# Half-array down products among the first queries and scores of a fused attention and GeGLU kernel

## The chip, the cores and the metric

The kernel runs on one core of a Trainium2 chip. The metric is the time of one execution on the device in microseconds (us). Engines are named TensorE (PE in the profile, its weight loads PEld), VectorE (DVE), ScalarE (ACT), GpSimd (POOL) and SyncE (SP); SyncE here only starts DMA transfers.

## The reference

For 2048 tokens of width 448: a layer norm, then two branches from the same normed rows, and a gated sum.

```python
xn = _layernorm(x, axis=-1)
# A: 16 query heads, 8 key/value heads, Dh = 256, the last W = 512 keys
q = (x @ wq).reshape(B, Sq, Hq, Dh).transpose(0, 2, 1, 3)
scores = jnp.einsum("bhqd,bhkd->bhqk", q, k) * (Dh ** -0.5)
o = jnp.einsum("bhqk,bhkd->bhqd", _softmax(scores, axis=-1), v)
s = o.transpose(0, 2, 1, 3).reshape(B, Sq, Hq * Dh) @ wo
# B: 448 -> 1792 -> 448
g = _silu((_gelu(xn @ w_gate) * (xn @ w_up)) @ w_down)
return x + s * g
```

## The kernel before, in words

**FFN.** The 2048 tokens are 16 tiles of 128, four tiles to a chunk of 512 columns. `gu_group` (L543) makes gate and up of 128 hidden features for one chunk, as pairs of 64-row products in the two row halves of TensorE; `gu_evac` (L558) takes them out of PSUM (gelu on ScalarE into `gl`, the product with up on VectorE into `actT[c % 2][:, f, :]`, f = 0 to 13). A down tile is 14 full 128-row products of `actT` and `wd`, 448 columns wide, into one PSUM bank (`down_mm`, L572), then the gate: tanh on ScalarE, `(tanh + 1) * sum` on VectorE (`down_gate`, L577), which `store_g` (L567) sends to DRAM by SyncE's queue. `down_tile` (L588) does a whole tile; `down` (L592) does tiles 0 to 3 and 4 to 7 among the gate and up groups. Tiles 8 to 15 are cut into pieces of 4 to 7 products by `down_piece` (L997) and set between the products of value and output weights of each head (`vw_head`, L732). Tile 14 sums in bank 0, tile 15 in bank 3.

**Attention.** The value cache times the output weights of each head is made beforehand (`vw`), so that a step only has to make queries, scores, softmax and `p @ vw`. There are 128 steps n: 8 blocks c of 256 queries, 16 heads h = n % 16 each. In step n TensorE makes the scores of step n (`s_jobs`, two tiles t, banks 4 to 6 in turn), the queries of step n + 2 (`q_jobs`; bank 7, and for steps 2 to 5 the second half of the head in bank 1) and the products with `vw` of step m = n - 4 (`pv_jobs`, `pv_plan`), as soon as n is 4. All of these are products of 64 rows; each list has a lower and an upper half (u = 0, 1), and `halves` (L799) merges the two lists by their columns so that both row halves of TensorE are fed in turn. TensorE takes its queue in order. Where one half writes a bank that the other half wrote before, `halves` makes it wait for the other's last product there.

The product with `vw` uses seven products in place of eight (a Strassen form). Its inputs are the transposed probabilities `pT` and four sums of them, `sS[0]` to `sS[3]`, that VectorE makes in the order 0, 2, 1, 3 (`sums`, L882). `AT` and `B0` to `B3` say which product goes to which of banks 0 to 3: product 7 reads `sS[2]`, product 6 reads `sS[1]`, both go to bank 1 (`B1`); product 3 reads `sS[3]` and goes to bank 3 (`B3`). The upper half of an ordinary step is queries, scores, then B1, B3, B2, B0; the lower half is the first scores, B0 and B2, queries, the second scores, B1, B3. `FIRST`, `LAST` and `TLAST` name the products that start and end a bank's sum.

The other engines run through the rest of a step in the order of the program (L1052 to L1117): VectorE's reciprocal of step n - 1 and GpSimd's two norms `pn`, a transposing DMA into `pT` by SyncE's queue, VectorE's row minimum of each tile (`row_min`), ScalarE's copy of the new queries (`q_evac`; in steps 0 to 3 VectorE copies the second half of the head from bank 1), ScalarE's exponential of each tile (`expo`), VectorE's sums of step n - 3. In the step where a block ends (h = 3, m % 16 == 15) the four banks are copied out (`evac`) and 13 end pieces (`finish`, L957: adds on GpSimd, multiplies with the gate on VectorE) are put on a list, from which each step takes one at its end (L1111).

**Around the change.** After the heads' `vw`: the queries of steps 0 and 1 in two calls of `halves` (L1026, L1027), a piece of four down products (L1051), and in each of steps 0 to 3 a piece of five at the step's end (L1098). Tile 14 ends in step 1, tile 15 in step 3; `store_g` comes at the start of steps 2 and 4 (L1057).

Of the kernel before, what the change touches and what calls it, by code (L numbers as in the profile page):

```python
# [13 lines left out]
P = 128  # L14
# [152 lines left out]
def bass_recurrent_scan__sliding_block_cached__geglu_ffn__prompt_kernel(  # L167
# [12 lines left out]
    _, S, D = A_x.shape  # L180
    Hkv, Sk, Dh = A_k_cache.shape[1], A_k_cache.shape[2], A_k_cache.shape[3]
    HD = A_wq.shape[1]
    Hq = HD // Dh
    W = min(4096, max(256, Sk // 4))
    F = B_w_gate.shape[1]
    NT = S // P
    QC = 512
    NQC = S // QC
    NF = F // P
    NJ = W // P  # L190
    NCO = HD // P
    R = 64
# [11 lines left out]
    with es:  # L204
# [367 lines left out]
        def down_mm(t, o, wr, f0, f1):  # L572
            c, t4 = divmod(t, 4)
            mms([(o, actT[c % 2][:, f, t4 * P:(t4 + 1) * P], wd[:, f, :], f == 0, f == NF - 1)
                 for f in range(f0, f1)], [b_wd] + b_actT[c % 2], wr)

        def down_gate(t, o, wr):  # L577
            s, y = t % 2, t % NG2
# [7 lines left out]
            keep_g.append((t, g, bg))  # L586

        def down_tile(t, o, wr):  # L588
            down_mm(t, o, wr, 0, NF)
            down_gate(t, o, wr)  # L590

        def down(c, pairs):  # L592
# [139 lines left out]
        def vw_head(h, banks, last=True):  # L732
            K.reuse(flat(b_vw[h]))
            for j, i in zip((0, 2, 1, 3), banks):
                vw_mm(h, j, i)
            if last:
                vw_sums(h)
# [61 lines left out]
        def halves(lo, up):  # L799


            t, todo = [0, 0], (list(lo), list(up))
            while todo[0] or todo[1]:
                u = 0 if todo[0] and (not todo[1] or t[0] <= t[1]) else 1
                i, c0, c1, l, r, st, sp, reads = todo[u].pop(0)
                t[u] += c1 - c0 + 6
                other = half_of[i][1 - u]
                half_of[i][u] = mms([(bank[i][:, c0:c1], l, r, st, sp)], reads, [b_ps[i]],
                                    [] if other is None else [other])
# [3 lines left out]
        def q_jobs(n, e):  # L813

            c, h = divmod(n, Hq)
            y, i = c % 2, bq(n)
            if e == 1 and 2 <= n < 2 + LAG:
                i = 1
            out = ([], [])
            for u in range(2):  # L820
                rows = slice(R * u, R * u + R)
                for k in [2, 1, 0] + ([NK] if u == e else []):
                    l = wqr[rows, h, :] if k == NK else wq[rows, k, h * Dh + e * P:h * Dh + (e + 1) * P]
                    out[u].append([i, e * CW, (e + 1) * CW, l, xq[rows, y, k, :], False, False,
                                   b_wql[h // HG] + [b_xq[y][k]]])
            return out
# [14 lines left out]
        def s_jobs(n, t, low_first):  # L841
            h, i = n % Hq, bs(n, t)
            s, g = n % NQT, h // 2
            out = ([], [])
            for u in range(2):
                rows = slice(R * u, R * u + R)
                for e in range(2):
                    out[u].append([i, 0, W, qT[rows, s, e, t * P:(t + 1) * P], kT[rows, g, e, :], False, False,
                                   [b_kT[g], b_qT[s][e]]])
            flag(*((out[0], out[1]) if low_first else (out[1], out[0])))  # L850
            return out

        def row_min(n, t):
            i = bs(n, t)
            m = (2 * n + t) % 8
            K.op("dve", lambda e: e.tensor_reduce(mn[:, m:m + 1], bank[i], AX.X, ALU.min), (b_ps[i],), (b_mn[m],))  # L856
# [25 lines left out]
        def sums(n, parts):  # L882
# [7 lines left out]
            for p in parts:  # L890
# [2 lines left out]
            return o  # L893

        AT = {1: (0, 0), 2: (0, 1), 6: (1, 0), 7: (1, 1), 4: (2, 0), 5: (2, 1), 3: (3, 0)}
        B0, B1, B2, B3 = (((1, 0), (1, 1), (2, 0), (2, 1)), ((6, 0), (6, 1), (7, 0), (7, 1)),
                          ((4, 0), (4, 1), (5, 0), (5, 1)), ((3, 0), (3, 1)))
        FIRST = {(0, (1, 0)), (0, (4, 0)), (0, (3, 0)), (1, (7, 0))}
        LAST = {(1, (2, 1)), (0, (7, 1)), (1, (5, 1)), (1, (3, 1))}
        TLAST = {(0, (2, 1)), (1, (7, 1)), (0, (5, 1)), (1, (3, 1))}  # L900

        def pv_src(n):
            x, y = n % NPT, n % NSS
# [15 lines left out]
        def pv_plan(n):  # L919
            if n % Hq == Hq - 1:  # L920
                one, mid, two, all_ = B0 + B2 + B1[:1], B3, B1[1:], B0 + B1 + B2 + B3
            elif n % Hq == 0:
                one, mid, two, all_ = B0 + B2, (), B3 + B1, B0[:2] + B1[2:] + B1[:2] + B0[2:] + B2 + B3
            else:
                one, mid, two, all_ = B0 + B2, (), B1 + B3, B1 + B3 + B2 + B0
            last = LAST if n % Hq == Hq - 1 else TLAST if n == NST - LAG - 1 else ()
            u = 0 if n + LAG + 2 < NST else 1
            return [pv_jobs(n, u, x, last) for x in (one, mid, two)] + [pv_jobs(n, 1 - u, all_, last)]
# [68 lines left out]
        def down_piece(n):  # L997
            while n:
                t, f = divmod(down_at[0], NF)
                k = min(n, NF - f)  # L1000
                i = 4 + t % 2 if t < NT - 2 else (0, 3)[t - NT + 2]
                down_mm(t, bank[i][:, 0:D], [b_ps[i]], f, f + k)
                down_at[0] += k
                n -= k
                if f + k == NF:
                    down_gate(t, bank[i][:, 0:D], [b_ps[i]])
                    if t < NT - 2:
                        store_g()
# [11 lines left out]
        vw_head(14, (1, 2, 3, 6))  # L1020
        down_piece(4)
        vw_head(15, (7, 1, 2, 3))
        js = [[q_jobs(n, e) for e in range(2)] for n in range(2)]
        js[0][0][1][0][5] = js[1][1][0][0][5] = True
        js[0][0][0][-1][6] = js[1][1][1][-1][6] = True
        halves(js[1][1][0] + js[1][0][0], js[0][0][1] + js[0][1][1])  # L1026
        halves(js[0][1][0] + js[0][0][0], js[1][0][1] + js[1][1][1])  # L1027
        K.reuse(flat(b_qT))
        for n in range(2):
            q_evac(n)  # L1030
# [17 lines left out]
            act(gsl[:, t, :], gr[:, y, :], ACT.Copy, (b_gr[y], b_sc), (b_gsl[t],), scale=sc[:, 1:2])  # L1048

        todo, stores, ready = [], [], []  # L1050
        down_piece(4)  # L1051
        for n in range(NST):  # L1052
            h, m = n % Hq, n - LAG
            c = n // Hq
            more = n + 2 < NST
            ends = m >= 0 and m % Hq == Hq - 1
            if n in (2, LAG):  # L1057
                store_g()
            if n == LAG:
                K.reuse(b_pT[3:] + b_sS[2])  # L1060
            s0, s1 = s_jobs(n, 0, True), s_jobs(n, 1, not more or m < 0)
            for t in ready:
                store_out(t)
            ready, stores = stores, []
            if moves and n < NST - 2:
                moves.pop(0)()
            if more:
                q0, q1 = q_jobs(n + 2, 0), q_jobs(n + 2, 1)
                q0[1][0][5] = q1[0][-1][6] = True
                if m < 0:  # L1070
                    q1[1][0][5] = q0[0][-1][6] = True
            if m < 0:
                halves(s0[0] + s1[0] + q0[0] + q1[0], q0[1] + q1[1] + s0[1] + s1[1])
            else:
                one, mid, two, all_ = pv_plan(m)
                if more:
                    halves(s0[0] + one + q0[0] + q1[0] + mid + s1[0] + two, q0[1] + q1[1] + s0[1] + s1[1] + all_)
                else:
                    halves(s0[0] + s1[0] + all_, one + s0[1] + s1[1] + two)
            if n >= 1:  # L1080
                recip(n - 1)
                norm(n - 1)
            row_min(n, 0)
            if more:
                q_evac(n + 2)
            if ends:
                evac(0, "dve")
                evac(2, "act")
            row_min(n, 1)
            expo(n, 0)  # L1090
            expo(n, 1)
            if 3 <= n < NST - 1:
                sums(n - 3, (0, 1))
                if ends:
                    evac(1, "dve")
                sums(n - 3, (2, 3))
            if n < LAG:
                down_piece(5)  # L1098
            if n in VW12:
                vw_plain(VW12[n])  # L1100
            if n == NST - 2:
                gates_scaled(0)
                gates_scaled(1)
            if n == LAG:
                K.reuse(b_aS + flat(b_tmp) + flat(b_ofin) + b_xr + b_gr)
                for t in range(NXR):
                    load_fin(t)
            if ends:
                evac(3, "act")
                todo.extend(finish(m // Hq, "pool"))  # L1110
            for _ in range(2 if n - NST + Hq in (8, 12) else 1):  # L1111
                if todo:
                    todo.pop(0)()
            if h == LAG and c >= 1 and c + 1 < NC:
                for k in range(NK + 1):
                    moves.append(lambda k=k, y=(c + 1) % 2, d=xnd[c + 1, :, k, :], r=b_xnd[2 * c + 2:2 * c + 4]: dma(
                        "sp", xq[:, y, k, :], d, r, (b_xq[y][k],)))  # L1117
# [120 lines left out]
```

## Time and profile before

| what | value |
|---|---|
| median of 3 runs | 555.11 us (554.72 to 555.96) |
| profiled execution, its own time | 554.54 us |
| its span, first to last instruction | 552.7 us |
| mean granted TensorE clock | 0.999 |
| TensorE busy | 545.0 us (99% of the span) |
| VectorE, ScalarE, GpSimd busy | 84%, 61%, 45% |
| full 128-row down products (`bank<-wd,actT`) | 224, 353 ns mean in the record |
| attention steps, first score to first score | 2.97 us in most |

A record of a product lasts longer than its share of TensorE, since products overlap in the pipe; the pace is read from start to start. In the timelines the columns are the start, the time taken, the engine, the line, the operation, output and input by the program's names, shapes, the number of instructions merged into the row (x), and in brackets the idle time before and what ended it. In the list of waits each row says who waited for whom, how long in all, how often, and the longest.

### The profile page before, as it was taken

What the parts mean: (1) busy time and instruction counts of PE and PEld (TensorE: products, weight loads), DVE (VectorE), ACT (ScalarE), POOL (GpSimd) and SP (SyncE); (2) the same over time, 40 slices, a digit from 0 to 9 for tenths busy, and PEclk for the clock granted to TensorE, in tenths of its full rate; (3) what the DMA queues carried; (4) which work ended last, traced back from release to release, by engine and by line L of the source; (5) the groups of instructions that cost most, each with busy time, mean ns of one, the idle gap of its engine ahead of it and who ended that gap; (6) DMA issues with size and microseconds to landing.
All of it is one profiled execution on the core that took longest, in us unless ns stands there. A gap on an engine that the chain in (4) does not pass through costs nothing.

```text
span 552.7 us, 18715 instructions
## 1 busy us (share of the span) xinstructions
PE 545.0 (99%) x7612; PEld 437.2 (79%) x7612; DVE 464.7 (84%) x1202; ACT 339.8 (61%) x809; POOL 249.8 (45%) x388
## 2 busy tenths in 40 slices
PE   8999999999999999999999999999999999999996
PEld 5544444445557999999999999999999999999983
DVE  6674979858867778988988898898989989889996
ACT  5432323467766666766767666676676666666753
POOL 1121590100004444655656456555555555564665
PEclk9999999999999999999999999999999999999999
DMA  9997999501106865556656875755677476576665
GB/s 270 184 239 147 210 317 179 115 1 36 46 8 102 140 114 88 103 96 116 116 105 104 132 101 95 121 114 107 107 118 107 93 135 108 94 114 115 94 103 86
DMA packets 190246, 66.07 MB, mean 120 GB/s; under 512 B 169408, under 2 KB 187984, under 8 KB 190160
## 3 DMA queue, kind: packets, MB, share of 16 engines
q1 hardware_dynamic: 186928, 56.96, 59.6%
q0 software_dynamic: 2464, 7.34, 4.5%
q8 instruction: 60, 0.98, 0.8%
q10 hardware_dynamic: 768, 0.57, 0.3%
q14 instruction: 26, 0.21, 0.1%
HBM read 19.76 MB, written 5.77 MB: 46 GB/s over the span
## 4 chain that ended last, share of the span: by engine, by line
PE 91%; DVE 5%; DMA 2%; issue 1%; ACT 1%; POOL 0%; SPq 0%; DVEq 0%; ACTq 0%
PE bank L387 91%; DVE mn L856 1%; DVE actT L562 1%; DMA x<-in_A_x_dram 1%; DMA pT<-pn 1%; DVE mx L679 1%; DVE sS L892 1%; DVE xn L460 0%; DVE stats L434 0%; ACT gl L381 0%; POOL rstd L446 0%; SPq L375 0%; ACT p L861 0%; DVE qT L832 0%; DVE p L1121 0%
## 5 line engine op out<-in xcount | busy, mean ns | idle before, releaser
L387 PE MATMUL bank<-kT,qT 64*128 64x512 bf16 x1024 | 281.4, 376 | 0.2
L877 POOL TENSOR_SCALAR pn<-p,rd 128x512 f16<-128x512 f32 x254 | 172.5, 691 | 225.6 <-DVE rd L867 225.6
L387 PE MATMUL bank<-vw,sS 64*128 64x224 f16 x1984 | 223.3, 256 | 0.2 <-DVE sS L892 0.2
L387 PE MATMUL bank<-xq,wq 64*128 64x256 bf16 x1536 | 221.9, 269 | 0.1
L387 PE MATMUL bank<-vw,pT 64*128 64x224 f16 (+1 forms) x1520 | 208.7, 258 | 0.7 <-DMA pT<-pn 0.7
L856 DVE TENSOR_REDUCE mn<-bank 128x1 f32<-128x512 f32 x256 | 173.7, 682 | 36.8 <-PE bank L387 34.6
L861 ACT ACTIVATE p<-bank,mn 128x512 f32<-128x512 f32 x256 | 174.9, 684 | 5.3 <-DVE mn L856 2.5
L387 PEld LDWEIGHTS bank<-vw,sS 64*128 64x128 f16 x1984 | 164.1, 94 | 7.9 <-DVE sS L892 2.5
L387 PEld LDWEIGHTS bank<-xq,wq 64*128 64x128 bf16 x1536 | 141.7, 94 | 10.0 <-PE bank L387 0.7
L381 ACT ACTIVATE qT<-bank 128x512 bf16<-128x512 f32 (+1 forms) x128 | 75.5, 590 | 117.1 <-PE bank L387 116.3
L387 PEld LDWEIGHTS bank<-vw,pT 64*128 64x128 f16 (+1 forms) x1520 | 142.5, 94 | 5.8 <-DMA pT<-pn 1.4
L387 PEld LDWEIGHTS bank<-kT,qT 64*128 64x128 bf16 x1024 | 95.1, 94 | 4.1 <-ACT p L861 1.5
L892 DVE TENSOR_TENSOR sS<-pT 128x256 f16<-128x256 f16 x248 | 86.3, 388 | 0.0
L387 PE MATMUL bank<-xnT,wgu 64*128 64x512 bf16 (+2 forms) x768 | 84.5, 350 | 0.8 <-DVE actT L562 0.3
L387 PE MATMUL bank<-xq,wqr 64*128 64x256 bf16 x256 | 68.4, 269 | 0.0
L387 PEld LDWEIGHTS bank<-xnT,wgu 64*128 64x128 bf16 x768 | 36.5, 94 | 38.5 <-issue 1.1
L381 ACT ACTIVATE gl<-bank 128x512 bf16<-128x512 f32 x56 | 33.1, 597 | 49.7 <-PE bank L387 41.2
L562 DVE TENSOR_TENSOR actT<-bank,gl 128x512 bf16<-128x512 f32 x56 | 37.4, 685 | 16.7 <-PE bank L387 16.0
L861 ACT ACTIVATION_READ_ACCUMULATOR p<-bank,mn 128x1 f32 x256 | 50.7, 198 | 0.0
L387 PE MATMUL bank<-wd,actT 128*128 128x448 bf16 x224 | 45.9, 353 | 0.6 <-DVE actT L562 0.5
L892 DVE TENSOR_TENSOR sS<-pT,sS 128x256 f16<-128x256 f16 x124 | 36.2, 292 | 4.3
L387 PEld LDWEIGHTS bank<-wd,actT 128*128 128x128 bf16 x224 | 21.3, 98 | 22.1 <-issue 1.5
(84 smaller groups left out, 421.6 us busy)
## 6 DMA issues: line engine op xcount, KB each, us to landing
wq<-in_A_wq_dram POOLq DMA_DIRECT2D x8, 384.0 KB, 7.7
woa<-in_A_wo_dram POOLq DMA_DIRECT2D x6, 448.0 KB, 5.7
pT<-pn SPq DMA_TRANSPOSE x129, 3.1
xn_t<-xnT SPq DMA_DIRECT2D x16, 128.0 KB, 3.7
xr<-in_A_x_dram SPq DMA_DIRECT2D x16, 112.0 KB, 2.6
gr<-gate_t SPq DMA_DIRECT2D x16, 112.0 KB, 2.7
out_dram<-ofin SPq DMA_DIRECT2D x16, 112.0 KB, 2.0
wd<-in_B_w_down_dram SPq DMA_DIRECT2D x1, 1568.0 KB, 7.9
```

The source lines that it names most:

```text
L381: K.op("act", lambda e, o=o, i=i: e.activation(o, i, func, scale=scale), reads, writes)
L387: ins = e.matmul(o, lhsT=l, rhs=r, start=st, stop=sp)
L562: K.op("dve", lambda e: e.tensor_tensor(actT[c % 2][:, f, :], bank[b + 1], gl[:, s, :], ALU.mult), (b_ps[b + 1], b_gl[s]), (b_actT[c % 2][ ...
L679: K.op("dve", lambda e: e.tensor_reduce(mx[:, i:i + 1], o, AX.XY, ALU.max, apply_absolute_value=True), (b,), (b_mx,))
L856: K.op("dve", lambda e: e.tensor_reduce(mn[:, m:m + 1], bank[i], AX.X, ALU.min), (b_ps[i],), (b_mn[m],))
L861: K.op("act", lambda e: e.activation(p32[:, z, :], bank[i], ACT.Exp, bias=mn[:, m:m + 1], scale=-1.0, accum_out=rsum[:, 2 * r + t:2 * r + ...
L877: K.op(engs[t], lambda e, o=o, i=i, s=s: e.tensor_scalar(o, i, s, 1.0, op0=ALU.mult, op1=ALU.mult), (b_p32[z], b_rd[r]), (b_pn[y][t],))
L892: o = K.op("dve", lambda e, i=i, a=a, b=b, f=f: e.tensor_tensor(s[i], a, b, f), r, (b_sS[y][i],))
```

## The change

Five things, with their lines in the kernel before.

1. `down_mm` waits only for the `actT` buffers of its own f, and `down_tile` calls it in two groups (12 and 2 products).
2. The products of f = 4 to 13 of tile 14 and all of tile 15 become 64-row products (`d_jobs`) in the lists of `halves`: one share with the first queries, one in each of steps 0 to 3. The two calls of `halves` for the first queries become one. The pieces at L1051 and L1098 go.
3. In steps 0 to 3 the lower half makes its second scores at its end, after the queries. The gates of tiles 14 and 15 stand between the two exponentials of steps 2 and 3, `store_g` moves to steps 3 and 4, and in step 3 the four sums of step 0 are spread between the row minima, the query copy and the exponentials.
4. `B1` begins with product 7 (`sS[2]`) in place of product 6 (`sS[1]`).
5. No end piece is taken in steps with h = 4; in the last block two are taken at h = 8, 10 and 12 (before: 8 and 12).

```diff
@@ down_mm, down_tile
-                 for f in range(f0, f1)], [b_wd] + b_actT[c % 2], wr)
+                 for f in range(f0, f1)], [b_wd] + b_actT[c % 2][f0:f1], wr)
...
-            down_mm(t, o, wr, 0, NF)
+            down_mm(t, o, wr, 0, NF - 2)
+            down_mm(t, o, wr, NF - 2, NF)
@@ banks
-        B0, B1, B2, B3 = (((1, 0), (1, 1), (2, 0), (2, 1)), ((6, 0), (6, 1), (7, 0), (7, 1)),
+        B0, B1, B2, B3 = (((1, 0), (1, 1), (2, 0), (2, 1)), ((7, 0), (7, 1), (6, 0), (6, 1)),
...
-        LAST = {(1, (2, 1)), (0, (7, 1)), (1, (5, 1)), (1, (3, 1))}
-        TLAST = {(0, (2, 1)), (1, (7, 1)), (0, (5, 1)), (1, (3, 1))}
+        LAST = {(1, (2, 1)), (0, (6, 1)), (1, (5, 1)), (1, (3, 1))}
+        TLAST = {(0, (2, 1)), (1, (6, 1)), (0, (5, 1)), (1, (3, 1))}
@@ pv_plan, h = 0
-                one, mid, two, all_ = B0 + B2, (), B3 + B1, B0[:2] + B1[2:] + B1[:2] + B0[2:] + B2 + B3
+                one, mid, two, all_ = B0 + B2, (), B3 + B1, B0[:2] + B1 + B0[2:] + B2 + B3
@@ before the steps
+        def d_jobs(u, t, f0, f1):
+            rows, (c, t4) = slice(R * u, R * u + R), divmod(t, 4)
+            return [[(0, 3)[t - NT + 2], 0, D, actT[c % 2][rows, f, t4 * P:(t4 + 1) * P], wd[rows, f, :],
+                     u == 1 and t == NT - 1 and f == 0, u == 1 and f == NF - 1, [b_wd, b_actT[c % 2][f]]]
+                    for f in range(f0, f1)]
+
+        DL = ((NT - 2, 4, 10), (NT - 2, 10, NF), (NT - 1, 0, 5), (NT - 1, 5, 10), (NT - 1, 10, NF))
+        DU = ((NT - 1, 0, 6), (NT - 1, 6, 10), (NT - 2, 4, 9), (NT - 2, 9, NF), (NT - 1, 10, NF))
         js = [[q_jobs(n, e) for e in range(2)] for n in range(2)]
-        js[0][0][1][0][5] = js[1][1][0][0][5] = True
-        js[0][0][0][-1][6] = js[1][1][1][-1][6] = True
-        halves(js[1][1][0] + js[1][0][0], js[0][0][1] + js[0][1][1])
-        halves(js[0][1][0] + js[0][0][0], js[1][0][1] + js[1][1][1])
+        for q0, q1 in js:
+            q0[1][0][5] = q1[0][-1][6] = True
+        low, up = [sum([q[u] for x in js for q in x], []) for u in range(2)]
+        halves(d_jobs(0, *DL[0]) + low, up + d_jobs(1, *DU[0]))
...
-        down_piece(4)
@@ the steps
-            if n in (2, LAG):
+            if n in (3, LAG):
                 store_g()
-            s0, s1 = s_jobs(n, 0, True), s_jobs(n, 1, not more or m < 0)
+            s0, s1 = s_jobs(n, 0, True), s_jobs(n, 1, not more)
...
-                halves(s0[0] + s1[0] + q0[0] + q1[0], q0[1] + q1[1] + s0[1] + s1[1])
+                halves(s0[0] + d_jobs(0, *DL[n + 1]) + q0[0] + q1[0] + s1[0], q0[1] + q1[1] + s0[1] + s1[1] + d_jobs(1, *DU[n + 1]))
...
             row_min(n, 0)
+            if n == 3:
+                sums(0, (0,))
             if more:
                 q_evac(n + 2)
...
             row_min(n, 1)
+            if n == 3:
+                sums(0, (1, 2))
             expo(n, 0)
+            if n in (2, 3):
+                i = (0, 3)[n - 2]
+                down_gate(NT - 4 + n, bank[i][:, 0:D], [b_ps[i]])
             expo(n, 1)
-            if 3 <= n < NST - 1:
+            if n == 3:
+                sums(0, (3,))
+            elif 3 < n < NST - 1:
                 sums(n - 3, (0, 1))
...
-            if n < LAG:
-                down_piece(5)
...
-            for _ in range(2 if n - NST + Hq in (8, 12) else 1):
+            for _ in range(0 if h == LAG else 2 if n - NST + Hq in (8, 10, 12) else 1):
```

## The prediction

> **What bounds the kernel now.** I read the page's busy shares first, then the chain of waits, then the timelines around the three places that the change touches. TensorE is busy 99% of the span, and the chain lies on it:
>
> ```profile
> PE 545.0 (99%) x7612; PEld 437.2 (79%) x7612; DVE 464.7 (84%) x1202; ACT 339.8 (61%) x809; POOL 249.8 (45%) x388
> PE 91%; DVE 5%; DMA 2%; issue 1%; ACT 1%; POOL 0%; SPq 0%; DVEq 0%; ACTq 0%
> ```
>
> So the question is where TensorE is not at its pace. Starts of successive products give the pace: 64-row products of 512 columns start every 0.216 us in each row half, those of 256 columns every 0.109, those of 224 every 0.096; full 128-row products of 448 columns every 0.189 (56 of them from 38.57 to 48.98). An ordinary attention step has in each half 4, 7 and 14 of the narrow ones: 0.86 + 0.77 + 1.34 = 2.97 us, and steps 6 to 18 take just that. There is nothing to win there. Off the pace are these.
>
> *FFN.* The second row of down tiles starts late; the waits put it down to VectorE:
>
> ```profile
> 64.36 0.68 DVE L562 TENSOR_TENSOR actT<-bank,gl 128x512 bf16<-128x512 f32 x1
> ...
> 65.09 0.49 PEld L387 LDWEIGHTS bank<-wd,actT 128*128 128x128 bf16 x4 [1.04 <-DVE actT L562]
> ```
>
> The last 512-column product before it starts at 64.18; the first down product at 65.10, 0.92 later. At the first row of tiles, which waits for nothing, that distance is 0.31 (38.26 to 38.57): 0.216 for the product, 0.093 to go from half-array to full-array products. The stall is 0.61 us.
>
> *Head of attention (157 to 178).* Full down products stand between half products, and each change of form costs:
>
> ```profile
> 161.73 1.12 PE L387 MATMUL bank<-wd,actT 128*128 128x448 bf16 x5
> 162.78 0.39 PE L387 MATMUL bank<-kT,qT 64*128 64x512 bf16 x1
> ```
>
> Five products at 0.189 are 0.95, the piece takes 1.05; about 0.1 goes at either end. Steps 0, 1 and 2 take 2.79 each, step 3 takes 3.37, because VectorE and ScalarE stand behind the gate of tile 14 (step 1).
>
> *Every 16 steps.* Starts of the steps around a block's end: 219.32, 222.39, 225.49, so step 20 takes 3.07, step 21 takes 3.10. The second excess is a wait for VectorE's sums:
>
> ```profile
> 222.73 1.16 DVE L892 TENSOR_TENSOR sS<-pT 128x256 f16<-128x256 f16 x2
> ...
> 223.04 0.69 POOL L963 TENSOR_TENSOR aS<-aS 128x224 f32<-128x224 f32 x1
> ...
> 223.81 0.28 DVE L892 TENSOR_TENSOR sS<-sS,pT 128x256 f16<-128x256 f16 x1
> ```
>
> Two sums took 1.08 us start to next start (0.40 in a quiet step, 216.56 to 216.96) while GpSimd ran an end piece. The third, done at 224.09, releases TensorE at 224.14, which could have started at 224.05 in the upper half and 224.02 in the lower.
>
> **A. Down in two groups (L588, L575).** The first 12 products now wait only for their own `actT` buffers (f up to 11, done at 61.5), the last 2 for f = 12 and 13, done at 65.04; they come 12 x 0.189 = 2.27 after 64.48. Banks: the first tile's was freed by the gelu of 61.31, the second's by VectorE at 63.93. Cover is ample: **-0.61**. What is late next? From 65 to 75 VectorE has 9.5 us of work in 11, but TensorE needs none of it until the next pair of banks. VectorE is late again at 105.05, at the end of a run of work fed by TensorE after 79.08; that run starts earlier by the same 0.61. Were it held by loads instead, up to 0.36 would come back at 105.
>
> A rule speaks on the down products. In rows, LDWEIGHTS of 98 ns stands inside the 0.189 pace of full products: nothing of it shows. The Trainium skill, "TensorE: Matmul & The Clock Gate", Part 3 (The mechanism), says that a weight load overlaps a running product only where the row group differs. By that an estimate would add 24 x 0.098 = 2.4 us of gain for the half products; the row denies it, and the sum takes none.
>
> **B. Half products (L1023 to L1098).** Removed: 24 full products (4 before step 0, 5 in each of steps 0 to 3), five changes of form each way, and the drain between the two groups of first queries (157.93 to 158.26, of which 0.22 is idle). Added: 24 products in each half, at 0.189 (no 64-row product of 448 columns is in the trace; bounds 0.096 of 224 and 0.216 of 512 columns; the full one has as many columns, so its pace). If the two halves did not run side by side it would be 24 x 0.189 = 4.5 us more; the 512-column products do.
> The first stage has per half 14 x 0.109 + 6 x 0.189 = 2.66, from 157.05, less what the upper half loses waiting for bank 7 (read by VectorE until 157.21, next product at 157.26): end 159.93. The first score waits for ScalarE's queries: last lower query about 159.04, ScalarE 0.30 after it (158.93 to 159.23 before), 0.60 long: step 0 at 160.00, as before, with two pairs more done.
> Steps 0 and 3: 4 x 0.216 + 7 x 0.109 + 4 x 0.189 = 2.39; steps 1 and 2, with five: 2.575. If nothing waits, step 4 starts at 160.00 + 9.92 = 169.92 instead of 171.73.
> What is late next, with these rows: row minimum 0.69 (0.60 to the next in a busy queue), expo 0.69 with 0.81 to VectorE's reciprocal, qT on VectorE 0.41, sum 0.20 to 0.31, tanh 0.53, gate 0.62. Reciprocals fall at 164.13, 166.71 and, since tanh of tile 14 (ends 168.84) stands ahead of the last expo of step 2, 169.62. Queries of the upper half in steps 2 and 3 find bank 1 read with hardly 0.01 to spare. Then on VectorE: minimum 169.70, first sum 170.30, qT, second minimum, two sums, gate of tile 15, last sum.
> The first sum now meets GpSimd's norms (169.9 to 171.26). The nearest row is the pair above, slowed by 0.68; nothing at best, 0.96 if both norms go first; I take 0.3, the rest of one norm. The Trainium skill, "SBUF — State Buffer", section "SBUF: two separate sides", has it that VectorE and GpSimd share a port pair as an exclusive lock and that the loser waits for the whole instruction. That is a rule against this place; by it the wait would be 0.28 or 0.96, and the head's gain 1.1 or about 0.5.
> Step 4 then waits thrice: 0.1 for bank 7 (ScalarE's qT ends 169.96), 0.2 for the second sum (172.0) at the upper half's first product in bank 1, 0.5 for the last sum (173.07) and the gate of tile 15 (172.86) at the lower half's first in bank 3, due at 172.62. Step 5: 169.92 + 2.97 + 0.8 = 173.69; step 6: 176.66 against 177.74 before. **-1.08**, between -1.9 (no waits) and -0.4 (waits of 1.5).
> Queues: SP's store of gate 14 moves behind step 2 and is issued about 169.9, its transposes at 168.4 and 171.3, so it holds none; that of gate 15 goes at 172.9, before 174.5. The transposes of step 0 leave at 165.9 and land after 3.1 (2.5 to 4.9): 169.0, needed at 170.3. tanh among exp loads no table (three loads in the whole trace). GpSimd gets nothing new here.
>
> **C. Bank 1 and end pieces (L896, L924, L1111).** The upper half's first product in bank 1 now needs the second sum (begun before 223.81, done by 223.89 if nothing else moved) rather than the third; the third is needed 2 x 0.096 later, at 224.24, and is there at 224.09. Leaving out step 4's piece also brings both sums forward by up to 0.68. Either alone removes the 0.13. Step 20's excess stays: there TensorE waits for ScalarE's expo behind the evacuation of bank 2 (220.60). Moving the 13 pieces one step puts the last GpSimd add into step 0 of the next block, whose slack for sums is 0.65; adds in steps 9 to 15 delay nothing now. In the last block two pieces go in step 10 too, so all end at step 13 as before; the tail (from 532.59 VectorE's chain, started by TensorE) only moves along. Seven blocks: **-0.91** (nothing to -1.7, all their excess).
>
> **Sum.** -0.61 - 1.08 - 0.91 = -2.60. The profiled execution took 554.54 (span 552.7): 551.9. Its own time is 0.57 under the median of the runs (555.11), which I take as scatter: 552.5 as a median.
>
> **Rivals.**
> 1. *The head gives its gain back* (waits in steps 2 to 4 of 1.8 rather than 0.8, banks 1, 7 and 3 found unread). For: 0.01 of room in bank 1. Against: in the old order step 3 waited just 0.58. Gain 1.6: 553.5. Chance 0.22.
> 2. *The stalls are only moved:* block ends wait elsewhere, VectorE's backlog at 105 returns 0.36, head 0.4. Gain 0.25 + 0.4 = 0.65: 554.5. For: VectorE is at 84%. Against: 0.5 idle in each ordinary step. Chance 0.11.
> 3. *Slower: the first sum waits for its transpose.* It sits in VectorE's queue ahead of bank 1's evacuation and the second minimum of step 3, so all stops if the transpose of step 0 is late. It costs nothing up to a landing of 4.4 us after issue (165.9 to 170.3), then 1 us per us; from 4.4 + 2.6 + 1.1 = 8.1 us the kernel is slower. At 9 us: 557.1. The longest landing is 4.9, so chance 0.05.
>
> **Numbers.** Forecast 552.5, chance 0.62 (its own bounds 550.8 to 553.3); range 550.8 to 554.3, which leaves out most of rivals 2 and 3. A measurement of this kernel tells 0.2% (1.1 us) from no change. Faster: forecast and rival 1, 0.84; same: rival 2, 0.11; slower: 0.05.
>
> **What will show it.** The second row of down tiles 0.31 after the last gate product; no 128-row product after the last value-weight product but the tail's; step 4 about 1.8 us after its old place against step 0, a wait at bank 3 in step 4; step 21 at 2.97, step 20 still near 3.07. Wrong would be: a first stage of over 3 us (halves not side by side), or a wait of VectorE for `pT` in step 3.

## The result and the profile after

| | before | changed |
|---|---|---|
| median of 6 runs each, side by side | 554.90 us | 552.72 us (552.09 to 553.50) |
| ratio | 1 | 0.9959, 95% interval 0.9946 to 0.9972 |
| profiled execution, its own time | 554.54 us | 553.09 us |
| its span | 552.7 us | 551.3 us |
| mean granted TensorE clock | 0.999 | 1.000 |

The kernel became 2.18 us faster (0.39% of 554.90). The forecast was 552.5, from a gain of 2.60 us; faster was given 0.84. From the page of the changed kernel, busy time by engine and the chain that ended last:

```profile
PE 542.9 (98%) x7636; PEld 441.2 (80%) x7636; DVE 462.5 (84%) x1202; ACT 339.9 (62%) x809; POOL 249.4 (45%) x388
PE 92%; DVE 3%; DMA 1%; issue 1%; POOL 0%; ACT 0%; SPq 0%; DVEq 0%; ACTq 0%; POOLq 0%
```

The page hardly moved: 24 products and weight loads more (24 of full height became 48 of half height), VectorE's share of the chain 3% in place of 5%. What follows is read from start to start, as the prediction did. In us; the starts are those of the products named, and a step lasts from its first score to the next step's first score:

| stretch | before | changed | difference |
|---|---|---|---|
| first down product | 38.57 | 39.76 | +1.19 later |
| first product of the second down row | 65.10 | 65.67 | +0.57 later |
| first product of the stage ahead of step 0 | 157.05 | 157.62 | +0.57 later |
| from there to step 0 | 2.95 | 2.99 | +0.04 |
| steps 0, 1, 2, 3 | 2.79, 2.79, 2.79, 3.37 | 2.39, 2.57, 2.63, 2.45 | -1.68 |
| steps 4, 5 | 2.98, 3.03 | 3.24, 3.05 | +0.28 |
| steps 20, 21, 23 | 3.07, 3.10, 2.97 | 3.06, 2.97, 2.98 | -0.13 |
| step 6 to step 112 | 316.32 | 315.56 | -0.76 |
| step 112 to step 127 | 44.86 | 44.83 | -0.03 |
| step 127 to the end | 13.83 | 13.96 | +0.13 |

So the three parts gave 0.61 (A: from the last gate product to the first down product 0.92 became 0.31), 1.35 (B) and 0.67 (C), together 2.63 us; and 1.19 us went the other way before 40 us, in a stretch that the change does not touch. That loss is taken up below; without it the execution agrees with the predicted sum.

**A.** The changed kernel's timeline of VectorE, TensorE and its weight loads where the second down row begins:

```profile
64.28 1.46 PE L387 MATMUL bank<-xnT,wgu 64*128 64x512 bf16 x12
...
65.54 0.68 DVE L562 TENSOR_TENSOR actT<-bank,gl 128x512 bf16<-128x512 f32 x1
65.67 0.30 PEld L387 LDWEIGHTS bank<-wd,actT 128*128 128x128 bf16 x3 [0.42 <-issue]
```

The down products now start while VectorE still makes the last `actT` (65.54 to 66.22); before, they started when it was done. The last gate product starts at 65.36, so the distance is the 0.31 of an undisturbed row. The 0.42 ahead of the weight load is no loss: it is the load engine's idle time while the gate products run.

**B.** The changed kernel's timeline of TensorE in the stage ahead of step 0:

```profile
157.62 0.36 PE L387 MATMUL bank<-wd,actT 64*128 64x448 bf16 x1
157.84 0.28 PE L387 MATMUL bank<-xq,wq 64*128 64x256 bf16 x1
157.84 0.36 PE L387 MATMUL bank<-wd,actT 64*128 64x448 bf16 x1
...
158.04 0.35 PE L387 MATMUL bank<-wd,actT 64*128 64x448 bf16 x1
...
158.23 0.35 PE L387 MATMUL bank<-wd,actT 64*128 64x448 bf16 x1
...
158.42 0.35 PE L387 MATMUL bank<-wd,actT 64*128 64x448 bf16 x1
```

The 448-column half products start 0.19 apart (157.84, 158.04, 158.23, 158.42), and between them the other half's queries start: side by side, at the pace that the sum took for them. And the wait that step 4 has in exchange, in the timeline of weight loads:

```profile
173.31 0.09 PEld L387 LDWEIGHTS bank<-vw,sS 64*128 64x128 f16 x1 [0.27 <-DVE sS L893]
173.31 0.09 PEld L387 LDWEIGHTS bank<-vw,pT 64*128 64x128 f16 x1
```

One wait of 0.27 for the last sum, in both halves at once. The prediction had three, of 0.8 together. VectorE's timeline shows why:

```profile
170.77 0.42 DVE L893 TENSOR_TENSOR sS<-pT 128x256 f16<-128x256 f16 x1
171.12 0.41 DVE L833 TENSOR_SCALAR qT<-bank 128x256 bf16<-128x256 f32 x1
171.45 0.67 DVE L857 TENSOR_REDUCE mn<-bank 128x1 f32<-128x512 f32 x1
172.05 0.27 DVE L893 TENSOR_TENSOR sS<-pT 128x256 f16<-128x256 f16 x1
172.25 0.28 DVE L893 TENSOR_TENSOR sS<-sS,pT 128x256 f16<-128x256 f16 x1
172.45 0.61 DVE L584 SCALAR_TENSOR_TENSOR g2r<-tmpr,bank 128x448 bf16<-128x448 f32 x1
172.98 0.28 DVE L893 TENSOR_TENSOR sS<-pT,sS 128x256 f16<-128x256 f16 x1
```

No row has an idle time in brackets: VectorE runs without a gap here. The first sum beside GpSimd's norms took 0.35 to the next start rather than 0.20, so 0.15 of slowing where 0.3 was taken. Less the 0.57 by which the stage starts later, the gate ends at 172.49 and the last sum at 172.69, where the prediction had 172.86 and 173.07: the queue runs 0.4 ahead of the one that I had drawn up.

**C.** The list of waits of TensorE's weight loads from 176 to 500 us. Before:

```profile
PEld bank L387 <- DVE sS L892: 1.5, 6, 0.2
PEld bank L387 <- ACT p L861: 1.0, 6, 0.2
```

After (total us, times, longest):

```profile
PEld bank L387 <- ACT p L862: 1.0, 6, 0.2
```

The wait for VectorE's sums is gone from all six blocks in that window; the one for ScalarE in step 20 stays as it was. VectorE in step 21 of the changed kernel:

```profile
221.94 0.69 DVE L893 TENSOR_TENSOR sS<-pT 128x256 f16<-128x256 f16 x2
222.56 0.28 DVE L893 TENSOR_TENSOR sS<-sS,pT 128x256 f16<-128x256 f16 x1
222.87 0.29 DVE L893 TENSOR_TENSOR sS<-pT,sS 128x256 f16<-128x256 f16 x1
```

The first two sums take 0.62 to the next start where they took 1.08: the end piece that slowed them runs a step later.

### The profile page after: what moved, and what is told of

Its sections match the earlier page's. It is cut to its first block, busy times and chain, and to the rows that moved or that the text cites. A ratio compares the mean times of both kernels' runs of the same rounds, so it can differ in the third digit from the quotient of the medians.

```text
span 551.3 us, 18761 instructions
## 1 busy us (share of the span) xinstructions
PE 542.9 (98%) x7636; PEld 441.2 (80%) x7636; DVE 462.5 (84%) x1202; ACT 339.9 (62%) x809; POOL 249.4 (45%) x388
## 4 chain that ended last, share of the span: by engine, by line
PE 92%; DVE 3%; DMA 1%; issue 1%; POOL 0%; ACT 0%; SPq 0%; DVEq 0%; ACTq 0%; POOLq 0%
PE bank L387 92%; DVE sS L893 1%; DMA x<-in_A_x_dram 1%; DVE mn L857 1%; DMA pT<-pn 1%; POOL pn L878 0%; DVE actT L562 0%; DVE mx L680 0%; ACT gl L381 0%; SPq L375 0%; DVE tmp L975 0%; DVE stats L434 0%; DVE p L1137 0%; DVE ofin L1137 0%; ACT xnT L381 0%
## 5 line engine op out<-in xcount | busy, mean ns | idle before, releaser
L387 PEld LDWEIGHTS bank<-vw,sS 64*128 64x128 f16 x1984 | 161.8, 94 | 5.7 <-DVE sS L893 1.1
L387 PE MATMUL bank<-wd,actT 128*128 128x448 bf16 (+1 forms) x248 | 51.2, 352 | 0.0
L387 PEld LDWEIGHTS bank<-wd,actT 128*128 128x128 bf16 (+1 forms) x248 | 23.5, 97 | 19.8 <-issue 1.2
```

The lines of the kernel that those rows point to most:

```text
L387: ins = e.matmul(o, lhsT=l, rhs=r, start=st, stop=sp)
```

## The experiments

The theory at the outset: the parts are independent, A is a stall taken away, B a shorter row of products less new waits for VectorE, C one wait that either of its two edits removes, and the 1.19 us before 40 us is scatter. The rivals: A and B only move VectorE's backlog; C's pieces hurt the tail; the early loss belongs to the change. Each edit is given against the kernel named with it; each ratio and each difference of medians is against the kernel before on the same chip, whose median was 554.75 for the first four, 554.91 for the next four and 554.69 for the last four.

**1. A alone** (against before).

```diff
-                 for f in range(f0, f1)], [b_wd] + b_actT[c % 2], wr)
+                 for f in range(f0, f1)], [b_wd] + b_actT[c % 2][f0:f1], wr)
...
-            down_mm(t, o, wr, 0, NF)
+            down_mm(t, o, wr, 0, NF - 2)
+            down_mm(t, o, wr, NF - 2, NF)
```

> Part A alone: the kernel before with down in two groups, each waiting only for its own actT buffers. Theory: the second row of down tiles starts 0.31 us after the last gate product instead of 0.92, and everything after it moves 0.61 us earlier; nothing else changes, so 0.6 us less than before (0.9989). Rival (VectorE's backlog at 105 us is bound by loads): up to 0.36 comes back at 105, leaving 0.25 us. The offset of the products after 105 us against the kernel before tells them apart.

Measured: 554.10, ratio 0.9989 (0.9980 to 0.9998), -0.65 us. Against before, TensorE is 0.67 us ahead at 65 us and 0.66 ahead at 178, of which 0.06 stood already at 38 us, before the edit acts. The gain stays; VectorE's run of work at 105 us takes none of it back.

**2. Bank 1's order alone** (against before; `LAST`, `TLAST` and `all_` follow from it).

```diff
-        B0, B1, B2, B3 = (((1, 0), (1, 1), (2, 0), (2, 1)), ((6, 0), (6, 1), (7, 0), (7, 1)),
+        B0, B1, B2, B3 = (((1, 0), (1, 1), (2, 0), (2, 1)), ((7, 0), (7, 1), (6, 0), (6, 1)),
```

> The order of bank 1 alone (product 7 before product 6); end pieces as before. Theory: the second sum is there before the upper half needs it, so steps 21, 37 and so on take 2.97 us instead of 3.10, seven times 0.13: 0.9 us less. Rival (the sums are late as a whole because GpSimd holds them up): the second sum is late too, steps 21 keep 3.0 or more, and less than 0.4 us is gained.

Measured: 553.91, 0.9984 (0.9975 to 0.9993), -0.84 us. Step 21 and its like take 2.97; the steps 20 of the later blocks take 3.09 to 3.11 in place of 3.07. Step 6 to step 112: 315.73 against 316.32. In the last block step 117 takes 2.97 in place of 3.18, but from step 112 to the end it is 58.73 in place of 58.69.

**3. No end piece in step 4 alone** (against before).

```diff
-            for _ in range(2 if n - NST + Hq in (8, 12) else 1):
+            for _ in range(0 if h == LAG else 2 if n - NST + Hq in (8, 10, 12) else 1):
```

> No end piece in steps with h = 4 alone; the order of bank 1 as before. Theory: the pair of sums of step 20 takes 0.4 to 0.6 us again instead of 1.08, the third sum is there in time, and steps 21 take 2.97: 0.9 us less, the same gain as the order of bank 1 alone gives, so the two are not additive. Rival (the lateness comes from the block's end, VectorE's copies): the pair is still late and steps 21 keep 3.05 or more. In the last block a VectorE piece moves one step nearer to the end; if VectorE bounds the tail, 0.1 to 0.3 us come back there, and step 126 takes over 3.0.

Measured: 554.45, 0.9994 (0.9985 to 1.0003): not to be told from no change by the time. The trace tells more: step 21 takes 2.97 here too, but step 23 takes 3.00, and in the last block steps 118, 119, 124 and 126 take 3.01, 3.04, 3.07 and 3.04 where all took 2.95 to 2.97. Step 6 to step 112 is 315.76. So either edit removes the 0.13 of step 21 for itself, as the prediction had it; but in the last block the 0.21 won in step 117 is lost again in the later steps (step 112 to 127: 44.94 in place of 44.86).

**4. B alone** (against before: `d_jobs`, the merged lists and the spread sums of the diff above, with A and C left out).

```diff
-        halves(js[1][1][0] + js[1][0][0], js[0][0][1] + js[0][1][1])
-        halves(js[0][1][0] + js[0][0][0], js[1][0][1] + js[1][1][1])
+        halves(d_jobs(0, *DL[0]) + low, up + d_jobs(1, *DU[0]))
...
-        down_piece(4)
...
-            if n < LAG:
-                down_piece(5)
```

> Part B alone: half products, gates and sums of the first steps as in the changed kernel, but down in one group, bank 1 and end pieces as before. Theory: from the first query product to the start of step 6 this is 1.3 to 1.4 us shorter than before (1.37 in the changed kernel), of which the changes of form are five times 0.19 and the drain between the two query groups 0.22; 1.3 us less in all. Rival (part B lives on the other parts: the second sum in step 4 would be late without the new order of bank 1): step 4 waits longer, gain 1.0 or less.

Measured: 553.28, 0.9973 (0.9963 to 0.9984), -1.47 us; in the profile TensorE goes from 0.12 ahead at 156.93 to 1.45 ahead at step 6, which is 1.33. Steps 0 to 5 take 2.39, 2.57, 2.63, 2.45, 3.25, 3.05, the same as in the changed kernel to 0.01. B owes nothing to the other parts, and step 4's wait is its own.

**5. The last block's pieces as before** (against changed).

```diff
-            for _ in range(0 if h == LAG else 2 if n - NST + Hq in (8, 10, 12) else 1):
+            for _ in range(0 if h == LAG and n < NST - Hq else 2 if n - NST + Hq in (8, 12) else 1):
```

> The changed kernel, but in the last block the end pieces are taken as before (one in step h = 4, two at h = 8 and 12), so that the VectorE piece of step 122 goes back to step 121. Theory: in the changed kernel VectorE is the chain from 525 us on, because its pieces stand nearer to the end; steps 118, 119 and 126 (2.99, 3.03, 3.06) go back to 2.97, 2.97, 2.95, and 0.1 to 0.25 us is gained. Rival: the tail's chain starts at its last step whatever comes before; no change.

Measured: 551.97, 0.9943 (0.9930 to 0.9955). Step 112 to 127 takes 44.70 in place of 44.83: step 126 is back at 2.90 (3.06), while steps 118 and 121 are at 3.01 and 3.02. From step 127 to the end it takes 13.99 in place of 13.96, so 0.1 us is left of it, less than medians can tell: in the profiles of the kernel before and of experiments 1, 4 and 12, which have the same last block, step 112 to the end takes 58.69 to 58.82. What the tail costs is not shown, but this is not where the time is.

**6. The early loss: stores of `xn_t` later** (against changed). In the changed kernel's queue of SyncE, between 20 and 27 us:

```profile
20.34 2.72 SPq L375 DMA_DIRECT2D xn_t<-xnT  x4
23.10 1.70 SPq L378 DMA_TRANSPOSE xnT<-xn  x1
24.85 0.58 SPq L375 DMA_DIRECT2D xn_t<-xnT  x1
25.48 1.32 SPq L378 DMA_TRANSPOSE xnT<-xn  x1
```

and in its timeline of TensorE:

```profile
27.77 1.48 PE L387 MATMUL bank<-xnT,wgu 64*128 64x512 bf16 x12
30.58 0.82 PE L387 MATMUL bank<-xnT,wgu 64*128 64x512 bf16 x6 [1.34 <-DVE actT L562]
```

The products at 30.58 read the last transposed tile. The wait names VectorE's `actT`, but TensorE needs the transposes of tiles 6 and 7 here, which stand in the queue behind four stores and one. The kernel before has, in the same two timelines:

```profile
25.03 1.32 SPq L378 DMA_TRANSPOSE xnT<-xn  x1
...
29.39 0.82 PE L387 MATMUL bank<-xnT,wgu 64*128 64x512 bf16 x6 [0.29 <-issue]
```

The trace also holds the moment at which a DMA lands, that is, when its last data have arrived. Tile 7's transpose lands at 30.49 in the changed kernel's profile and at 29.30 in the one before; the products start 0.09 us later in both, and just as long after it in the nine other profiles that leave the stores where they were.

```diff
-            store_xn()
+            if n >= 10:
+                store_xn(max(2, len(keep_xn) - 2))
```

> The changed kernel, but the stores of the normed rows to DRAM start with the group of feature 10 and go two at a time, so that the transposes of tiles 6 and 7 do not stand behind them in SyncE's queue. Theory: TensorE's wait at 29 us (0.46 us in the profile before, about 1.5 us in the profile of the changed kernel) is for the transpose of tile 7, issued behind five stores; without them it is issued near 24.3 instead of 25.0 to 25.5, the wait shrinks to 0 to 0.5 and 0.5 to 1.0 us is gained; the scatter from run to run shrinks as well. Rival: the transpose lands late because the transfers share the DMA engines with the weight loads; then the wait stays.

Measured: 551.65, 0.9938 (0.9926 to 0.9951); all runs between 551.33 and 551.78. The changed kernel's own spread over 1.4 us, but that the spread shrinks by this edit is not shown: experiments 5 and 8, with the stores in their old place, spread over 0.52 and 0.35, and experiment 10, with them moved, over 0.95. SyncE's queue in this kernel:

```profile
19.71 0.58 SPq L375 DMA_DIRECT2D x<-in_A_x_dram  x1
21.49 4.21 SPq L378 DMA_TRANSPOSE xnT<-xn  x2
```

Both transposes are issued between 21.49 and 25.70, and from 20 to 38 us the list of waits holds no row of TensorE any more, where the changed kernel has 1.8 us for the weight load and 1.3 for the product. Tile 7's transpose now lands at 28.52. The cause of the wait is the transposes, and not `actT`, which this edit leaves alone. The edit moves the stores' issue and their transfers at once, so what the transfers do to the transposes is not told apart.

**7. The four sums of step 0 after both exponentials** (against changed).

```diff
             row_min(n, 0)
-            if n == 3:
-                sums(0, (0,))
...
-            if n == 3:
-                sums(0, (1, 2))
...
-            if n == 3:
-                sums(0, (3,))
-            elif 3 < n < NST - 1:
+            if 3 <= n < NST - 1:
```

> The changed kernel, but the four sums of step 0 stand together after both exponentials of step 3, behind the gate of tile 15, as the old program had them. Theory: the second sum ends near 173.2 instead of 172.3 against a need at 172.5, the last near 173.7: the wait in step 4 grows from 0.27 to 0.7 or 0.8, so 0.4 to 0.5 us more than the changed kernel. Rival: the early sum costs as much by meeting GpSimd's norms (0.35 instead of 0.20 us in the changed kernel) as it gains; no difference.

Measured: 553.21, 0.9969 (0.9959 to 0.9979). Step 4 takes 4.41 in place of 3.24, and step 5 is back at 2.97. This kernel's timeline of VectorE, one row of ScalarE's and one of the weight loads, and then its list of waits for weight loads from 165 to 178 us:

```profile
171.97 0.68 DVE L857 TENSOR_REDUCE mn<-bank 128x1 f32<-128x512 f32 x1
173.08 0.62 DVE L584 SCALAR_TENSOR_TENSOR g2r<-tmpr,bank 128x448 bf16<-128x448 f32 x1 [0.43 <-PE bank L387]
173.62 0.48 DVE L893 TENSOR_TENSOR sS<-pT 128x256 f16<-128x256 f16 x2
...
172.44 0.54 ACT L381 ACTIVATE tmpr<-bank 128x448 f32<-128x448 f32 x1
...
173.96 0.09 PEld L387 LDWEIGHTS bank<-vw,sS 64*128 64x128 f16 x1 [1.49 <-DVE sS L893]
```

```profile
PEld bank L387 <- DVE sS L893: 1.5, 1, 1.5
```

The direction is as expected, the size over twice that: steps 4 and 5 together take 1.09 more. The sums themselves end where I had put them: this profile stands 0.87 behind the changed kernel's first one at step 0, and less that the second ends at 173.2 and the last at 173.8. What I had left out is the need for the first sum. The lower half's product 5 reads it (`sS[0]`) in `B2`, right after the products with `pT`: in the changed kernel that weight load starts at 171.57, here at 173.96, when the first sum, begun at 173.62, is done, and TensorE waits 1.5 us. Part of the lateness is a gap of 0.43 on VectorE ahead of the gate; its row names TensorE, but the gate needs ScalarE's tanh, which runs from 172.44 to 172.98. In the changed order two of the sums stand in that place.

**8. Step 20's excess: bank 2 copied out after the first exponential** (against changed).

```diff
-                one, mid, two, all_ = B0 + B2, (), B3 + B1, B0[:2] + B1 + B0[2:] + B2 + B3
+                one, mid, two, all_ = B0, B2, B3 + B1, B0[:2] + B1 + B0[2:] + B2 + B3
...
-                evac(2, "act")
...
+            if ends:
+                evac(2, "act")
```

> The changed kernel, but at a block's end ScalarE copies bank 2 out after the first exponential instead of before it, and in the next step the lower half makes its bank 2 products after the queries. Theory: the 0.10 us that step 20 still takes too long is TensorE's wait for the exponential of step 19, which stands behind that copy; steps 20 then take 2.97, seven times 0.10: 0.7 us less than the changed kernel. Rival: the copy is then late for bank 2 and the wait only changes its name.

Measured: 552.49, 0.9955 (0.9943 to 0.9967). Step 20 takes 3.15, not 2.97. In this kernel's list of waits from 176 to 500 us:

```profile
PEld bank L387 <- PE bank L387: 1.4, 6, 0.2
```

The wait for ScalarE is gone and one half now waits for the other in the same bank, six times 0.2: 1.4 us in place of 1.0. The rival was right: the 0.10 of step 20 is not to be had by this exchange.

**9. The changed kernel once more**, with nothing altered, to see what of 552.72 is scatter.

> The changed kernel once more, beside the next three. Theory: its first profile lost 1.06 us at 29 us, where nothing was changed (TensorE waiting for the transpose of tile 7); that wait is scatter, so here the products after 105 us stand 0.6 us ahead of the kernel before, and the time is 552.0 to 552.3, about 2.6 us less than before. Rival (the wait belongs to the changed kernel): 552.7 again.

Measured: 551.75 (551.54 to 552.82), 0.9949 (0.9936 to 0.9963), -2.94 us. Its profiled execution took 551.54, span 549.7. At 29 us it is 0.33 *ahead* of before, at 65 us 0.95 ahead; every step has its length from the first profile to 0.02. So two executions of the same program stand 1.5 us apart at 29 us, and from step 0 to step 127 the distance stays between 1.49 and 1.52. The time is even 0.25 below the least that I had expected: in its profile that wait is shorter than in the one before.

**10. Best of the findings:** changed, with experiments 5 and 6 together.

> The changed kernel with the two edits that gained: end pieces of the last block as before, and the stores of normed rows after the transposes. Theory: the gains add, 0.1 in the tail and 0.45 at 29 us, so 551.5 to 551.6, about 3.3 us less than before. Rival (the tail's time was scatter): as the later stores alone, 551.65.

Measured: 551.38 (551.30 to 552.25), 0.9939 (0.9927 to 0.9952), -3.31 us: the fastest kernel here, though its interval overlaps that of the changed kernel beside it. TensorE is 0.50 ahead at 29 us and 1.12 ahead at 65.

**11. Of part C only bank 1's order** (against changed: pieces by the old rule everywhere).

```diff
-            for _ in range(0 if h == LAG else 2 if n - NST + Hq in (8, 10, 12) else 1):
+            for _ in range(2 if n - NST + Hq in (8, 12) else 1):
```

> The changed kernel with the end pieces taken as before in all blocks, so that only the order of bank 1 is left of part C. Theory: the order of bank 1 alone keeps steps 21 at 2.97; steps 20 take 3.10 instead of 3.07 (six times 0.03 more), the tail gets back 0.1; 0 to 0.15 us more than the changed kernel, which makes the skipped piece worth nothing by itself. Rival: with the sums 0.3 later steps 21 wait again, 0.5 us or more.

Measured: 552.23, 0.9953 (0.9941 to 0.9966). Step 21 stays at 2.97, so the order alone removes its wait. But in five of the six blocks another step, the ninth (steps 40, 56 and so on), now takes 3.06 in place of 2.97, and waits for sums are back in the list from 176 to 500 us:

```profile
PEld bank L387 <- ACT p L862: 1.1, 6, 0.2
PEld bank L387 <- DVE sS L893: 0.5, 3, 0.2
```

Step 6 to 112 takes 316.06 against 315.59 in experiment 9, and from there to the end 0.04 comes back. The median is 0.48 above that of experiment 9, where I had expected 0.15 at most (the two intervals overlap, so this rests on the 0.47 of the traces): the piece left out is worth something in the full kernel, but through another step than the one it was meant for. Why the ninth step is open: experiment 2, with the same order and the same pieces, has its excess in step 20 instead.

**12. The later stores in the kernel before** (the edit of experiment 6, against before).

> The kernel before with only the later stores of normed rows. Theory: the wait at 29 us is in both kernels and has nothing to do with the change, so the same 0.46 us goes here, and with it the scatter; 554.3 against 554.8. Rival: in the old order VectorE's backlog at 65 us takes it back, since there TensorE waits for VectorE and not for its own pace: no change.

Measured: 554.17, 0.9990 (0.9981 to 0.9998), -0.5 us; TensorE 0.44 ahead at 29 us and still at 65. The wait is in the old kernel too. It is not something that the change brought.

## Why the prediction was right, and where its sizes were off

**A, right to the hundredth.** Forecast -0.61, read off the profile -0.61, by itself -0.65 by the medians and 0.61 by the trace. That nothing is late next until 105 us was the doubtful part; experiment 1 shows the gain whole at 178 us.

**B, right in its mechanism, with its waits put too high.** The rows of products came out as worked: steps 0 and 1 at 2.39 and 2.57, step 0 at 160.04 by the old start against 160.00, the half products at 0.19. Two terms were off. The thin room at bank 1 in steps 2 and 3 cost 0.06 in each, which rival 1 had feared to be more and the sum had at nothing. And "step 4 then waits thrice", 0.8 us, became 0.27 in step 4 and 0.08 more than an undisturbed step in step 5; the waits for bank 7 and for the second sum did not come. Together 0.47 where 0.8 stood. Gain 1.35 by the profile and, alone, 1.33 by the profile and 1.47 by the medians, against 1.08. Experiment 7 shows that the order on VectorE, the early first sum above all, is what keeps the waits so small.

The first sum beside the norms was slowed by 0.15. The Trainium skill, "SBUF — State Buffer", section "SBUF: two separate sides", would have the loser of the shared port pair wait for the other's whole instruction: 0.28 or 0.96 by the prediction's rows. The changed kernel's own rows give 0.28 again: two norms in 1.39 us from 170.36, the sum from 170.77. The measurement is smaller than either, and GpSimd's spans are too rough to say when the norm let go; the rule's sign holds, its size isn't what these rows show. The other rule that was weighed, the Trainium skill, "TensorE: Matmul & The Clock Gate", Part 3 (The mechanism), would have made B worth 2.4 us more, 3.5; experiment 4's 1.47 decides against reading it so.

**C, right in its mechanism, put too high.** "Either alone removes the 0.13" is shown for step 21 by experiments 2 and 3, and step 20's excess stayed. Between steps 6 and 112 six blocks gave 0.76, near six times 0.13; the seventh gave nothing. Two clauses failed. "All end at step 13 as before, the tail only moves along": in the changed kernel the chain of waits lies on VectorE from 525.00 to the end of the steps, before from 532.61. From the two chains, before and then changed:

```profile
510.85 21.74 PE bank L387 x305
...
532.61 0.69 DVE mn L856
```

```profile
173.31 351.66 PE bank L387 x4840
...
525.00 0.69 DVE mn L857
525.69 1.14 DVE sS L893 x3
```

That is 26.3 us before the end in place of 20.1; with the last block's pieces as before (experiment 5) it is 20.2 again. The pieces that were put off meet the sums of the last steps there; steps 119 and 126 take 3.03 and 3.06, and the 0.21 won in step 117 is gone by the end. The pieces are not the whole of it, since in experiment 2, which does not move them, it is gone as well. That this profile ends a further 0.1 later is not more than like profiles differ by (experiment 5). And "adds delay nothing" in later steps: step 23 takes 0.01 more, in experiment 3 even 0.03, and experiment 11's ninth step shows that with the pieces at their old places too a wait for sums can appear where the kernel before had none. So 0.67 in place of 0.91.

**The sum.** The errors of B (0.27 too little) and C (0.24 too much) cancelled: 2.63 against 2.60. That the total came out so near is in part luck, each of these two being off by a quarter of a microsecond.

**The median.** The profile that the first comparison rests on had lost 1.19 us at 29 us, a stretch which the change does not touch; experiments 6, 9 and 12 show that it is a wait for a transposing DMA behind stores in SyncE's queue, that it is in both kernels, and that its length differs from execution to execution. Medians of 552.72 and 551.75 for one and the same kernel, gains of 2.18 and 2.94, lie on either side of the forecast. Of the 1.5 us between the two profiles of the changed kernel 0.53 is a later issue (25.48 against 24.95) and 0.99 a longer way from issue to landing (5.01 against 4.02). Why the way differs is open.

**The rivals.** The head did not give its gain back (steps 2 to 5 lost 0.47, not 1.8). The stalls were not only moved; only the last block's 0.21 was. The first sum did not wait for its transpose: its row has no idle time.

## What to carry to other kernels

Read an engine that is 98% busy by the distance from start to start of its instructions, not by busy time: all three gains were made of stalls or changes of form of 0.1 to 0.6 us, and the busy share was 99% before and 98% after. When work is put off to take it out of one step, look at where the list ends, since the last block has no later step to hide it in. And before a difference of 1 us is credited to an edit, align the two traces instruction by instruction: here the largest single shift lay in a stretch that the edit did not touch.

## What the runs showed that I had not expected

- The releaser in a list of waits can be the wrong one for a DMA: the 1.34 us at 30.58 were put down to VectorE's `actT`, though TensorE started 0.09 after the transpose landed, and went away when two transposes were issued earlier.
- Four stores hold SyncE's queue for 2.7 us by being issued. With them moved behind, the transpose of tile 6 was issued at 21.49 in place of 23.10, that of tile 7 at 24.52 in place of 25.48.
- Two edits that each remove the wait of step 21 are not interchangeable with both: between steps 6 and 112 each alone gave 0.59 and 0.57 us, both together 0.76, and with the piece put back 0.47 was lost again.
- One wait less in a block's end (experiment 8) brought one of the same size between the two halves of TensorE, so what is read as a wait for an engine may have another right behind it.
